# Q turned on VectorE in 32x32 squares instead of on TensorE, for half of the groups, and one piece of a late split moved

## The chip, the cores and the metric

The kernel runs on one core of a Trainium2 chip. The metric is the device time of one execution in microseconds; lower is better. The profile is of one execution, taken by the hardware profiler, with the core's five instruction streams: PE (TensorE; PEld is its weight load), DVE (VectorE), ACT (ScalarE), POOL (GpSimd) and SP (SyncE, which here only issues DMAs).

## The reference

A delta-rule attention, then two feed-forward parts on its output:

```
q, k, v: (4, 8, 768, 48)   beta: (4, 8, 768)
k_n = k / (norm(k) + 1e-6);  state = 0
for t in range(768):
    y[t]  = q[t] @ state
    v_old = k_n[t] @ state
    state = state + beta[t] * outer(k_n[t], v[t] - v_old)
x = y laid out as (3072, 384)
x = (s * relu(x @ w_in)**2 + b) @ w_out            # 384 -> 2048 -> 384
e = argmax of the normalised x against 8 expert embeddings, with a softmax gate
out = gate * (relu(x @ w1[e]) @ w2[e])             # 384 -> 1024 -> 384, by expert
```

## The kernel before

The 768 positions are cut into 24 chunks of 32, and these into six groups (`gi` 0 to 5) of four chunks (`s` 0 to 3). Inside a group each chunk takes three steps on PE, with DVE between them: `ks` (state times k and q, tile `ch`, L307), `tx` (tile `u`, L328), and `ku` with `mu` (tiles `ds`, L344, and `ch`, L363). DVE makes `X`, `bdu` and the state `sst` from them. One step is a "hop"; a group has twelve, and each hop is cut in four. While group `gi` runs, the next one, `g2 = gi + 1`, is prepared: its loads are queued, k and q are turned so that the head dimension lies on the partitions (tile `kqt`, one for each chunk), `gram` multiplies k by k and q (tile `gr`, L220), and DVE inverts a 32x32 triangle (`lanes_1` to `lanes_3`, `solve`).

The first feed-forward part (`moe1`, tiles `h`, `r`, `gh`, `gl`, `acc`) is cut into small pieces that fill PE between the hops; its rows are written in the same program order. `attention` keeps a list of items with the hop at which each is due:

```
                for f in (tr_k, tr_q, gram):
                    for s in range(0, HG, 2 if f is gram else 1):
                        add(h, f, g2, s)
                        h += 0.25
```

with `h` starting at 3.25. So the order on PE, DVE, ACT and POOL is the order of the code; the order on SP's queue is set by a scheduler.

`tr_k` (L152) turns k of one chunk: four PE transposes into a PSUM tile `pp`, one ACT copy into `kqt`. It reads `kpad`, which 32 small DMAs fill (L117), and is due at hops 3.25 to 4. `tr_q` (through `tr_n`, L166 and L171) turns q of one head: four PE transposes of 128x112 into `pp`, four ACT copies. It reads `qpad`, filled by eight DMAs for a group (L125), and is due at 4.25 to 5; `gram` follows at 5.25 and 5.5. `qpad` is one buffer, `kpad` and `v` are two.

The last part (L1003, L917) runs over six blocks of 512 tokens, `s_`, each with four quarters `t`. In a quarter PE runs two pieces of the next block's first product (`ffn1`, tile `h`) and the second product of one quarter (`ffn2`, tile `o`). `x2_split` makes the high and low halves `x2h` (ACT, L992) and `x2l` (POOL, L993) of the block after next, in three pieces `m`, each behind a quarter: piece `t - 1` behind quarter `t`. `ffn1` of a block reads the pieces in the order 0, 1, 2.

Of the kernel before, what the change touches and what calls it, by code (L numbers as in the profile page):

```python
# [6 lines left out]
F32 = mybir.dt.float32  # L7
# [7 lines left out]
C = 32  # L15
HG = 4
# [3 lines left out]
def tile_kernel(ctx, tc, q, k, v, beta, w_in, w_out, s_in, b_in, emb, tau, w1, w2, out):  # L20
    nc = tc.nc
    B, H, S, D = q.shape
# [8 lines left out]
    DP = 2 * 64 - 16  # L31
# [6 lines left out]
    NST = NT // ST  # L38
# [5 lines left out]
    att = tc.alloc_tile_pool(name="att", bufs=1, side="right")  # L44
# [40 lines left out]
    qpad = att.tile([128, B, 4, DP], F32, name="qpad")  # L85
# [21 lines left out]
    v_t, kqt_t, mt_t, beta_t, tt_t, gc_t, x_t = {}, {}, {}, {}, {}, {}, {}  # L107
    KQB, MTB = 6, 6
# [37 lines left out]
                    in_=beta[h, 2 * r:2 * r + 2, gi * HG * C:(gi + 1) * HG * C].rearrange("g (n t) -> g n t", t=C))  # L146

    def tr_k(gi, s, eng=None):
        kqt_t[gi, s] = att.tile([128, B, 256], F32, tag="kqt", name="kqt", bufs=KQB)[0:DP]
        pp = ps_pp.tile([128, B, 128], F32, tag="pp", name="pp")  # L150
        for h in range(B):
            nc.tensor.transpose(out=pp[0:DP, h, :], in_=kpad[gi % 2][:, h, s, 0:DP], identity=ident)  # L152
        o = kqt_t[gi, s].rearrange("p h (a x t) -> p (h a) x t", a=2, x=4)[:, :, 0::3, :]
        i = pp[0:DP].rearrange("p h (a x t) -> p (h a) x t", a=2, x=2)
        if eng is nc.vector:
            nc.vector.tensor_copy(out=o, in_=i)
        else:
            nc.scalar.copy(out=o, in_=i)

    def tr_n(gi, h, t, x, engines):  # L160
        if (gi, 0) not in kqt_t:
            for s in range(HG):
                kqt_t[gi, s] = att.tile([128, B, 256], F32, tag="kqt", name="kqt", bufs=KQB)[0:DP]
        pp = ps_pp.tile([128, 4, HG, C], F32, tag="pp", name="pp")
        for r in range(4):
            nc.tensor.transpose(out=pp[0:DP, r].rearrange("p n t -> p (n t)"), in_=t[:, h, r, 0:DP], identity=ident)  # L166
        for s in range(HG):
            o = kqt_t[gi, s][:, h].rearrange("p (a x t) -> p a x t", a=2, x=4)[:, :, x, :]
            i = pp[0:DP, :, s, :].rearrange("p (a x) t -> p a x t", a=2)
            if engines[s % len(engines)] is nc.scalar:  # L170
                nc.scalar.copy(out=o, in_=i)  # L171
            else:
                nc.vector.tensor_copy(out=o, in_=i)
# [3 lines left out]

    def tr_q(gi, h):
        tr_n(gi, h, qpad, slice(1, 3), (nc.scalar,))

    def k_rows(gi, s):
        pp = ps_pp.tile([128, B, DP], F32, tag="pp", name="kr")
        for h in range(B):
            for r in range(4):
                c = r // 2 * 128 + r % 2 * 96
                nc.tensor.matmul(out=pp[32 * r:32 * r + 32, h, :], lhsT=kqt_t[gi, s][:, h, c:c + 32],
                                 rhs=ident[0:DP, 0:DP], start=True, stop=True)
        nc.scalar.copy(out=kpad[gi][:, :, s, :], in_=pp)
# [225 lines left out]
    def attention(more, first):  # L414
        for gi in range(NG):
            items = []

            def add(h, f, *a):
                items.append((h, len(items), f, a))

            if gi == 0:
                add(0, first)
                for i in range(1, 3 * HG - 1):
                    add(i, x_step)
                add(10, x_step)
            if gi + 1 < NG:
                g2 = gi + 1
                sy = [nc.sync]
                if gi:
                    add(0, load_k, g2, sy)  # L430
                    add(0, load_n, g2, qpad, q, nc.sync)
                    add(0, load_beta, g2)
                    add(0, load_v, g2, nc.sync)
                h = 3.25
                if gi:
                    for f in (tr_k, tr_q, gram):
                        for s in range(0, HG, 2 if f is gram else 1):
                            add(h, f, g2, s)
                            h += 0.25
                else:  # L440
                    add(99, second_places)
                    for f in (tr_k, tr_q, gram):
                        for s in range(0, HG, 2 if f is gram else 1):
                            add(99 if f is tr_k and s < 2 else 100, f, 1, s)
                if gi:
                    for f, a in ((lanes_1, ()), (lanes_2, ()), (lanes_3, ()), (scale_v, (0, nc.vector)),
                                 (scale_v, (1, nc.vector))):
                        add(h, f, g2, *a)
                        h += 0.25
                    he = 11.25  # L450
                    for j in range(C - 1):
                        add(h + (he - h) * j / (C - 1), solve, g2, j)
                    add(he + 0.25, lanes_out, g2)
                else:
                    add(100, router_setup_a2)
                    add(200, lanes_1, 1)
                    add(200, lanes_2, 1)
                    add(200, lanes_3, 1)
                    add(201, scale_v, 1, 0, nc.vector)
                    add(201, scale_v, 1, 1, nc.vector)  # L460
                    add(201, router_setup_b)
                    for j in range(C - 1):
                        add(301 if j % 3 == 2 else 300, solve, 1, j)
                    add(400, lanes_out, 1)
            items.sort(key=lambda x: (min(x[0], 300) if x[0] > 100 else x[0], x[1]))

            def due(t):
                while items and items[0][0] <= t:
                    it = items.pop(0)
                    it[2](*it[3])  # L470

            hops = 0
            for s in range(HG):
                for _ in dstep(gi, s, more):
                    for i in range(4):
                        due(hops + i / 4)
                        st["hop"] += 0.25
                        st["gi"], n = gi, 4 * hops + i
                        w = [(2 if gi == 1 else 1.5) if x >= 23 else 1 for x in range(n, 4 * NS)]
                        st["left"] = sum(w) / w[0]  # L480
                        yield
                    hops += 1
            while items:
                it = items.pop(0)
                it[2](*it[3])
                if it[0] >= 100:
                    yield PREP[it[0]]
        st["hop"] += 100
# [311 lines left out]
    with tc.manual_schedule(engines={ET.PE, ET.DVE, ET.Activation, ET.Pool}):  # L800
# [28 lines left out]
        for s in range(HG):  # L829
            gram_first(0, s, ga)  # L830
            if s % 2:
                for g in range(2):
                    o = gc_t[0][:, :, g, s - 1:s + 1, :]
# [11 lines left out]
        for h in range(B):  # L845
            tr_q(0, h)
# [137 lines left out]
        def x2_split(s_, m):  # L984
            if m == 0:
                xr_t[s_] = xs_t[s_]
                xs_t[s_] = (p2.tile([128, KD, ST], F32R, tag="x2h", name="x2h", bufs=2),
                            p2.tile([128, KD, ST], F32R, tag="x2l", name="x2l", bufs=2))
            xr = xr_t[s_]
            xh, xl = xs_t[s_]  # L990
            o = xh[:, m].rearrange("p (u t) -> p u t", u=NTS)
            nc.scalar.copy(out=o, in_=xr[:, :, m, :])  # L992
            nc.gpsimd.tensor_tensor(  # L993
                out=xl[:, m].rearrange("p (u t) -> p u t", u=NTS), in0=xr[:, :, m, :],
                in1=o.bitcast(F32), op=ALU.subtract)
# [159 lines left out]
        for s_ in range(NST):  # L1155
            if s_ + 2 < NST:
                x2_load(s_ + 2)
            for t in range(NTS):
                if s_ + 1 < NST:
                    ffn1(s_ + 1, 2 * t)  # L1160
                    ffn1(s_ + 1, 2 * t + 1)
                ffn2(s_, t)
                if s_ + 2 < NST and t:
                    x2_split(s_ + 2, t - 1)
                if (s_, t) == (0, 0):
                    router2b()
                for _ in range(2):
                    if nr < NTILE:
                        router3(nr)
                        nr += 1  # L1170
                if nr == NTILE:
                    router4()
                    nr += 1
                    pair_load(0)
                if s_ == NST - 1 and t < NTS - 1:
                    for f in range(KF2 // 2):
                        if t < 2:
                            pair_1(t * KF2 // 2 + f)
                    if t == 2:
                        pair_2()  # L1180
                        pair_out()
                        pair_last()
# [39 lines left out]
```

## Time and profile before

| | us |
|---|---|
| median of 3 runs (lowest, highest) | 921.82 (917.24, 922.56) |
| the profiled execution | 918.63 |
| its span, first to last instruction | 916.8 |
| PE busy in the span | 839.4 (92%) |
| DVE busy | 465.3 (51%) |
| ACT busy | 458.4 (50%) |
| POOL busy | 61.9 (7%) |

The busy times say which engine is full on the whole. The sums behind them are made against the profiled execution: 918.63 us, of which 1.83 us lie outside the span.

### The profile page before, as it was taken

The page shows a single profiled execution, that of the slowest core. Times are in us where ns is not written, and L with a number is a line of the kernel's source. Part 1 is how long each engine was busy: PE and PEld are TensorE (multiplying, and loading weights), DVE is VectorE, ACT ScalarE, POOL GpSimd, SP SyncE. Part 2 cuts the span into 40 slices and gives each one's busy share as a digit, 9 for nine tenths or more (in the row PEclk, how much of TensorE's full clock was granted, in tenths as well). Part 3 has the DMA queues.
Part 4 walks back from the last instruction along what each step waited for, and adds up shares of the span by engine and source line. Part 5 has one row for each costly group of instructions (what it writes and reads, how often), then busy time and mean ns, then how long its engine had stood idle before and what let it go on. Part 6 is the DMA issues. An engine that isn't in the chain of part 4 may idle for free. (4 is left out here: it accounts for less than half of the span.)

```text
span 916.8 us, 27694 instructions
## 1 busy us (share of the span) xinstructions
PE 839.4 (92%) x12090; PEld 770.5 (84%) x12090; DVE 465.3 (51%) x1051; ACT 458.4 (50%) x861; POOL 61.9 (7%) x71
## 2 busy tenths in 40 slices
PE   6467797876999999999999999999999999999996
PEld 4345686775989999999999999999997889889895
DVE  2979588669537942795368632225215423321101
ACT  1544646733575567565756566678653222222211
POOL 5115400000000000000000000000001011011000
PEclk7557899877999999999999999999999999999999
DMA  8683114211220222022000000015002910132000
GB/s 162 195 310 65 28 26 75 48 23 25 47 57 4 47 44 54 3 41 49 20 4 20 3 19 2 19 34 157 19 1 53 56 61 18 60 122 102 26 26 27
DMA packets 115593, 49.42 MB, mean 54 GB/s; under 512 B 89943, under 2 KB 112144, under 8 KB 115472
## 3 DMA queue, kind: packets, MB, share of 16 engines
q1 hardware_dynamic: 108560, 46.44, 22.4%
q10 hardware_dynamic: 6336, 1.18, 0.9%
q8 instruction: 95, 1.56, 0.7%
q14 instruction: 26, 0.21, 0.1%
q0 software_dynamic: 576, 0.02, 0.1%
HBM read 38.06 MB, written 9.74 MB: 52 GB/s over the span
## 5 line engine op out<-in xcount | busy, mean ns | idle before, releaser
L672 PE MATMUL acc<-gh,wp 128*128 128x256 f32 x1056 | 145.4, 284 | 0.0
L672 PEld LDWEIGHTS acc<-gh,wp 128*128 128x128 f32 x1056 | 132.6, 192 | 1.4
L635 ACT ACTIVATE r<-h 128x512 f32<-128x512 f32 x96 | 57.7, 601 | 130.5 <-PE h L627 103.4
L627 PE MATMUL h<-xh,wp 128*128 128x256 f32 x576 | 118.7, 289 | 2.4 <-ACT r L635 1.2
L627 PE MATMUL h<-xhl,wp 128*128 128x256 f32 x720 | 102.2, 287 | 0.0
L627 PEld LDWEIGHTS h<-xh,wp 128*128 128x128 f32 x576 | 94.5, 191 | 3.7 <-ACT r L635 1.6
L920 DVE SCALAR_TENSOR_TENSOR hl<-h,hh 128x512 fp32r<-128x512 f32 x46 | 31.8, 690 | 121.0 <-ACT hh L919 121.0
L649 DVE TENSOR_TENSOR gl<-r,gh 128x512 fp32r<-128x512 f32 x88 | 60.3, 685 | 62.4 <-ACT gh L647 62.4
L627 PEld LDWEIGHTS h<-xhl,wp 128*128 128x128 f32 x720 | 90.4, 189 | 1.1
L627 PE MATMUL h<-xl,wp 128*128 128x256 f32 x288 | 81.0, 281 | 0.0
L672 PE MATMUL acc<-gl,wp 128*128 128x256 f32 x528 | 76.3, 280 | 1.1 <-issue 1.1
L646 ACT ACTIVATE r<-r,b_sb,s_sb 128x512 f32<-128x512 f32 x88 | 72.0, 818 | 2.2
L377 ACT COPY x<-ch 32x384 f32<-32x384 f32 x96 | 45.2, 471 | 48.6 <-PE ch L363 47.5
L672 PEld LDWEIGHTS acc<-gl,wp 128*128 128x128 f32 x528 | 67.8, 190 | 1.3 <-issue 1.2
L289 DVE TENSOR_TENSOR T<-T,tmp 128x31 f32<-128x31 f32 (+15 forms) x186 | 65.1, 350 | 6.4
L993 POOL TENSOR_TENSOR x2l<-xr,x2h 128x512 fp32r<-128x512 f32 x15 | 19.4, 1291 | 719.4 <-DVE L L1090 592.7
L286 DVE TENSOR_TENSOR tmp<-A,T 128x31 f32<-128x31 f32 (+15 forms) x186 | 64.6, 348 | 5.0
L1003 PE MATMUL o<-w2h,hh 128*128 128x384 f32 x184 | 62.6, 340 | 0.0
L636 ACT ACTIVATE r<-r 128x512 f32<-128x512 f32 x96 | 60.7, 632 | 3.1
L1003 PE MATMUL o<-w2h,hl 128*128 128x384 f32 x184 | 62.2, 338 | 0.0
L1003 PE MATMUL o<-w2l,hh 128*128 128x384 f32 x184 | 62.1, 337 | 0.0
L1007 ACT ACTIVATE o<-o,gate 128x384 f32<-128x384 f32 x24 | 14.0, 582 | 94.1 <-PE o L1003 85.3
(215 smaller groups left out, 1437.9 us busy)
## 6 DMA issues: line engine op xcount, KB each, us to landing
wr<-in_moe_w_in SPq DMA_DIRECT2D x16, 384.0 KB
wr<-in_moe_w_out SPq DMA_DIRECT2D x8, 768.0 KB
v<-in_v SPq DMA_DIRECT2D x192, 24.0 KB
x2d<-x2s SPq DMA_DIRECT2D x24, 192.0 KB
out<-o SPq DMA_DIRECT2D x24, 192.0 KB
kpad<-in_k SPq DMA_DIRECT2D x160, 24.0 KB
qpad<-in_q SPq DMA_DIRECT2D x40, 96.0 KB
xr<-x2d SPq DMA_DIRECT2D x5, 768.0 KB
```

The source lines that it names most:

```text
L286: nc.vector.tensor_tensor(out=tmp, in0=A[:, j + 1:, j:j + 1].to_broadcast([128, m, j + 1]), in1=T[:, j:j + 1, 0:j + 1].to_broadcast([128, ...
L289: nc.vector.tensor_tensor(out=T[:, j + 1:, 0:j + 1], in0=T[:, j + 1:, 0:j + 1], in1=tmp, op=ALU.subtract)
L377: nc.scalar.copy(out=x_t[gi][pb:pb + C, :, r * 96:(r + 1) * 96].rearrange("p h (g e) -> p h g e", g=2), in_=y[32 * rr:32 * rr + 32, :, :, ...
L627: nc.tensor.matmul(out=h[:, f, :], lhsT=wi_(w, 2 * j + f, m), rhs=x[:, m, :], start=(m == 0 and i == 0), stop=(m == KD - 1 and i == 2))
L635: nc.scalar.activation(out=r, in_=h, func=AF.Relu)
L636: nc.scalar.activation(out=r, in_=r, func=AF.Square)
L646: nc.scalar.activation(out=r, in_=r, func=AF.Identity, scale=s_sb, bias=b_sb)
L649: later.append((step[0] + 11, lambda: nc.vector.tensor_tensor(out=gl, in0=r, in1=gh.bitcast(F32), op=ALU.subtract)))
L672: nc.tensor.matmul(out=acc[:, m * TT:(m + 1) * TT], lhsT=wo_(w, 2 * j + f, m * 128, 128) if kk else wx_(2 * j + 1, 2 * j + f, m * 128), rh ...
L920: nc.vector.scalar_tensor_tensor(out=hl, in0=ps, scalar=0.0, in1=hh.bitcast(F32), op0=ALU.max, op1=ALU.subtract)
L993: nc.gpsimd.tensor_tensor(out=xl[:, m].rearrange("p (u t) -> p u t", u=NTS), in0=xr[:, :, m, :], in1=o.bitcast(F32), op=ALU.subtract)
L1003: nc.tensor.matmul(out=ps, lhsT=h[:, sl], rhs=w[:, f, :], start=(f == 0 and i == 0), stop=(f == KF2 - 1 and i == 2))
```

## The change

For groups of index 3, 4 and 5 the q of a group is no longer loaded as eight DMAs of all 128 positions. `load_qb` loads each head in four bands: a band is 32 partitions of `qpad` (one half of the head pair `g`, one half `b` of the 48 dimensions), with the 32 positions of a chunk on the partitions and 32 or 16 of the dimensions as columns. That is 16 DMAs a head, 64 a group. `qpad` is seen as three slots, so head 3 shares a slot with head 0. `tr_qb` turns a head with four DVE transposes, one for each chunk, straight into `kqt`: no `pp` tile, no PE transpose and no ACT copy. Heads 0 to 2 are due at hops 3.75, 4 and 4.25, head 3 at hop 5; its load is put in at hop 4.25. `tr_k` starts at hop 2.75 in these groups instead of 3.25; `gram` stays at 5.25. In the last part the third piece of `x2_split` follows quarter 2, together with the second piece, and no longer quarter 3.

```
+    qn = qpad.rearrange("p h r d -> p (h r d)")[:, 0:3 * HG * 128].rearrange(
+        "p (h s r d) -> p h s r d", h=3, s=HG, r=4)
+    kqf_t = {}
+
+    def load_qb(gi, h):
+        for g in range(2):
+            for b in range(2):
+                w = min(32, D - 32 * b)
+                for s in range(HG):
+                    t = (gi * HG + s) * C
+                    nc.sync.dma_start(
+                        out=qn[32 * (2 * g + b):32 * (2 * g + b) + 32, h % 3, s, :, 0:w],
+                        in_=q[h, g::2, t:t + C, 32 * b:32 * b + w].rearrange("r t d -> t r d"))
+
+    def tr_qb(gi, h):
+        for s in range(HG):
+            o = kqf_t[s][:, h].rearrange("p (a x t) -> p a x t", a=2, x=4)[:, :, 1:3, :]
+            nc.vector.transpose(out=o, in_=qn[:, h % 3, s].rearrange("p (a x) d -> p a x d", a=2))
...
-                    add(0, load_n, g2, qpad, q, nc.sync)
+                    if g2 < 3:
+                        add(0, load_n, g2, qpad, q, nc.sync)
+                    else:
+                        for x in range(3):
+                            add(0, load_qb, g2, x)
+                        add(4.25, load_qb, g2, 3)
...
                 if gi:
-                    for f in (tr_k, tr_q, gram):
+                    if g2 > 2:
+                        h = 2.75
+                    for f in (tr_k, tr_qb if g2 > 2 else tr_q, gram):
                         for s in range(0, HG, 2 if f is gram else 1):
+                            if f is tr_qb and s == 3:
+                                h = 5
                             add(h, f, g2, s)
                             h += 0.25
...
                 ffn2(s_, t)
-                if s_ + 2 < NST and t:
-                    x2_split(s_ + 2, t - 1)
+                if s_ + 2 < NST:
+                    for m in ((), (0,), (1, 2), ())[t]:
+                        x2_split(s_ + 2, m)
```

On PE, while group 4 is prepared (`gi` 3), this stood around `tx` and the q turns before; `kpad` rows are `tr_k`, `qpad` rows `tr_q`:

```order
L672 MATMUL acc<-gl,wp_2569 128x256 x6
L152 MATMUL pp<-ident,kpad_103 112x128 x4
L627 MATMUL h<-xhl,wp_1957 128x256 x9
L328 MATMUL u<-X,tt 32x48 x32
L152 MATMUL pp<-ident,kpad_103 112x128 x4
L627 MATMUL h<-xhl,wp_1957 128x256 x3
L696 MATMUL lg<-x2s 128x136 x6
L627 MATMUL h<-xhl,wp_1957 128x256 x6
L166 MATMUL pp<-ident,qpad 112x128 x4
L672 MATMUL acc<-gh,wp_1976 128x256 x9
L166 MATMUL pp<-ident,qpad 112x128 x4
L672 MATMUL acc<-gh,wp_1976 128x256 x3
```

The same place on PE now:

```order
L701 MATMUL acc<-gl,wp_2569 128x256 x6
L656 MATMUL h<-xhl,wp_1957 128x256 x9
L348 MATMUL u<-X,tt 32x48 x32
L656 MATMUL h<-xhl,wp_1957 128x256 x3
L725 MATMUL lg<-x2s 128x136 x6
L656 MATMUL h<-xhl,wp_1957 128x256 x6
L701 MATMUL acc<-gh,wp_1976 128x256 x12
```

And the stretch on PE that begins two pieces earlier, where the k turns stand now:

```order
L701 MATMUL acc<-gl,wp_2471 128x256 x6
L153 MATMUL pp<-ident,kpad_103 112x128 x4
L656 MATMUL h<-xhl,wp_1947 128x256 x9
L327 MATMUL ch<-sst,kqt 64x48 x32
L153 MATMUL pp<-ident,kpad_103 112x128 x4
L656 MATMUL h<-xhl,wp_1947 128x256 x9
L153 MATMUL pp<-ident,kpad_103 112x128 x4
```

The q turns are gone and the twelve `acc` rows stand together; the first k turn stands in front of the `h` piece ahead of `ch`, where it stood behind the `h` piece after `ch`.

On DVE, the same preparation, from `X` to the mask of `gram`, before:

```order
L313 TENSOR_TENSOR X<-v,ch 128x384 x2
L649 TENSOR_TENSOR gl<-r,gh 128x512
L333 TENSOR_TENSOR bdu<-u,par 128x384 x2
L649 TENSOR_TENSOR gl<-r,gh 128x512
L699 TENSOR_TENSOR sq_5493<-lg,ident 128x256
L702 COPY LG<-lg 128x16
L703 TENSOR_REDUCE SS<-sq_5493 128x2
L352 TENSOR_TENSOR sst<-ds,sst 112x4x96 x2
L649 TENSOR_TENSOR gl<-r,gh 128x512
L204 TENSOR_TENSOR mt<-gr,mask_su 128x8x32 x4
```

And now, from the `gl` behind `X`:

```order
L678 TENSOR_TENSOR gl<-r,gh 128x512
L199 STREAM_TRANSPOSE kqt<-qpad 128x2x64 x4
L353 TENSOR_TENSOR bdu<-u,par 128x384 x2
L199 STREAM_TRANSPOSE kqt<-qpad 128x2x64 x4
L678 TENSOR_TENSOR gl<-r,gh 128x512
L728 TENSOR_TENSOR sq_5577<-lg,ident 128x256
L731 COPY LG<-lg 128x16
L732 TENSOR_REDUCE SS<-sq_5577 128x2
L199 STREAM_TRANSPOSE kqt<-qpad 128x2x64 x4
L372 TENSOR_TENSOR sst<-ds,sst 112x4x96 x2
L199 STREAM_TRANSPOSE kqt<-qpad 128x2x64 x4
L678 TENSOR_TENSOR gl<-r,gh 128x512
```

Each head is a block of four transposes: one ahead of `bdu`, one behind it, one ahead of `sst` and, for head 3, one behind `sst`.

On SP, from the loads of group 3 (`v`, `kpad`) to those of group 4, before:

```order
L135 DMA v<-in_v 32x4x48 x19
L117 DMA kpad_104<-in_k 32x4x48 x32
L135 DMA v<-in_v 32x4x48 x13
L688 DMA x2d<-x2s 128x3x128 x2
L125 DMA qpad<-in_q 128x4x48 x8
L924 TENSOR_LOAD esel
L924 ISA x2
L144 DMA beta<-in_beta 8x1x32 x16
L135 DMA v<-in_v 32x4x48 x7
```

And now, up to the second band of group 4's q:

```order
L135 DMA v<-in_v 32x4x48 x19
L117 DMA kpad_104<-in_k 32x4x48 x32
L135 DMA v<-in_v 32x4x48 x13
L192 DMA qpad<-in_q 32x4x32 x4
L192 DMA qpad<-in_q 32x4x16 x4
L192 DMA qpad<-in_q 32x4x32
L717 DMA x2d<-x2s 128x3x128 x2
L192 DMA qpad<-in_q 32x4x32 x3
L192 DMA qpad<-in_q 32x4x16 x4
L192 DMA qpad<-in_q 32x4x32 x4
L192 DMA qpad<-in_q 32x4x16 x4
```

Behind `v` stand first the sixteen loads of group 3's head 3, nine ahead of the `x2d` stores and seven behind them, and then the 48 loads of group 4's heads 0 to 2, still ahead of the next `beta` and `v`.

## Rows read from the trace of the kernel before

**Rows 1.** Busy time by engine in one preparation; last columns: PEclk, DMA share, GB/s.

```profile
260.00:356.00 96.00, 94.29 (x1799) 90.55 (x1798) 58.92 (x142) 59.69 (x115) 0.00 (x0) 1.00 0.19 36
```

**Rows 2.** Timeline of PE, group 4: start, length, what, count.

```profile
342.34 1.54 PE L672 MATMUL acc<-gh,wp 128*128 128x256 f32 x12
343.72 0.84 PE L672 MATMUL acc<-gl,wp 128*128 128x256 f32 x6
344.40 1.22 PE L627 MATMUL h<-xhl,wp 128*128 128x256 f32 x9
...
356.21 0.60 PE L166 MATMUL pp<-ident,qpad 128*112 128x128 f32 x4
356.57 1.30 PE L672 MATMUL acc<-gh,wp 128*128 128x256 f32 x9
...
358.06 0.60 PE L672 MATMUL acc<-gh,wp 128*128 128x256 f32 x3
358.49 0.85 PE L672 MATMUL acc<-gl,wp 128*128 128x256 f32 x6
```

**Rows 3.** Timeline of PE in the four stalls of the last part, the first of them.

```profile
744.03 0.49 PE L917 MATMUL h<-x2h,w1h 128*128 128x512 f32 x1
745.38 0.50 PE L917 MATMUL h<-x2l,w1h 128*128 128x512 f32 x1 [0.84 <-POOL x2l L993]
745.71 0.40 PE L917 MATMUL h<-x2h,w1l 128*128 128x512 f32 x1
745.95 0.39 PE L917 MATMUL h<-x2h,w1h 128*128 128x512 f32 x1
```

**Rows 4.** Timeline of POOL and of ACT at the splits.

```profile
744.06 1.26 POOL L993 TENSOR_TENSOR x2l<-xr,x2h 128x512 fp32r<-128x512 f32 x1 [7.15 <-ACT x2h L992]
```

```profile
769.86 0.61 ACT L992 CAST x2h<-xr 128x512 fp32r<-128x512 f32 x1
771.43 0.60 ACT L919 ACTIVATE hh<-h 128x512 fp32r<-128x512 f32 x1 [0.95 <-PE h L917]
```

**Rows 5.** DVE's transposes by line: count, ns min/median/max, first and last start.

```profile
L241 DVE STREAM_TRANSPOSE A<-gc x6: 1936/1992/2078, 20.7 to 466.4; 128x1024 f32<-128x1024 f32 x6
```

```profile
L276 DVE STREAM_TRANSPOSE nmc<-nm x6: 204/205/205, 26.7 to 474.5; 128x32 f32<-128x32 f32 x6
```

**Rows 6.** Timeline of DVE, groups 3 and 4; in brackets the idle time before.

```profile
251.47 0.68 DVE L649 TENSOR_TENSOR gl<-r,gh 128x512 fp32r<-128x512 f32 x1
```

```profile
353.40 1.02 DVE L333 TENSOR_TENSOR bdu<-u,par 128x384 f32<-128x384 f32 x2 [5.01 <-PE u L328]
...
361.70 1.02 DVE L352 TENSOR_TENSOR sst<-ds,sst 112x384 f32<-112x384 f32 x2 [5.13 <-PE ds L344]
```

**Rows 7.** Timeline of SP's queue from group 3's q to group 4's k.

```profile
179.37 5.93 SPq L125 DMA_DIRECT2D qpad<-in_q  x8
200.08 10.38 SPq L144 DMA_DIRECT2D beta<-in_beta  x16
215.99 10.32 SPq L135 DMA_DIRECT2D v<-in_v  x19
226.41 18.45 SPq L117 DMA_DIRECT2D kpad<-in_k  x32
...
258.05 1.24 SPq L688 DMA_DIRECT2D x2d<-x2s  x2
...
304.54 3.74 SPq L135 DMA_DIRECT2D v<-in_v  x7
...
322.95 17.05 SPq L117 DMA_DIRECT2D kpad<-in_k  x32
```

**Rows 8.** DMA issues with a time to landing: KB each, median us.

```profile
beta<-in_beta POOLq DMA_DIRECT2D x16, 1.0 KB, 3.7
```

**Rows 9.** Timeline of PE, group 3: the unit ahead of the k turns, and gram.

```profile
248.17 1.22 PE L627 MATMUL h<-xhl,wp 128*128 128x256 f32 x9
```

```profile
268.15 1.48 PE L220 MATMUL gr<-kqt 48*32 48x64 f32 x128
```

More of the change, by code (lines that the diff above doesn't have):

```diff
@@ L148, in tr_k @@
     def tr_k(gi, s, eng=None):
-        kqt_t[gi, s] = att.tile([128, B, 256], F32, tag="kqt", name="kqt", bufs=KQB)[0:DP]
+        kqf_t[s] = att.tile([128, B, 256], F32, tag="kqt", name="kqt", bufs=KQB)
+        kqt_t[gi, s] = kqf_t[s][0:DP]
         pp = ps_pp.tile([128, B, 128], F32, tag="pp", name="pp")
```

## The prediction

> **What bounds the kernel now.** I read the busy times by engine first, then PE's timeline, then the queues that feed it. In a whole preparation (260 to 356 us) PE is busy 94.3 of 96 us at a granted clock of 1.00, full speed (2.4 GHz); DVE is busy 58.9, ACT 59.7 [rows 1]. So in the groups that the change touches, PE's own instructions set the time, and what is taken from PE there shortens the kernel unless a new wait takes its place. In the last part PE stands still at four places for one reason: the second matmul of the third piece of a block waits for POOL's `x2l` [rows 3]. These two, PE time and that wait, are what the change can win. What can take it back is SP, which issues its DMAs one behind the other [rows 7].
>
> **Part 1, the q turns leave PE.** A turn is four transposes. Twelve `acc` matmuls without turns take from 342.34 to 343.72, 1.38 us. The same twelve, cut by two turns, take from 356.21 to 358.49, 2.28 us [rows 2]. So a turn costs PE 0.45 us, of which 0.36 is its own slot (356.21 to 356.57) and the rest the matmul behind it. Four turns a group, three groups: 12 x 0.45 = **5.4 us**, all of it in a stretch where PE is full. The lower bound is the slots alone, 12 x 0.36 = 4.3. The ACT copies behind the turns also go; ACT is not the bound and I count nothing for them.
>
> **What DVE gets.** 16 transposes a group of 128 columns on 128 partitions. No row has this size, but two lie around it: 32 columns take 205 ns, 1024 take 1992 [rows 5]. A line through them gives 1.80 ns a column and 0.38 us for one, 1.5 us for a head's block of four, 6.0 us a group. The bounds are 0.2 and 2.0 us; I take the line, since both rows are the same operation on the same type. Block by block: head 0's stands ahead of `bdu`, before which DVE is idle 5.01 us; head 2's ahead of `sst`, idle 5.13 [rows 6]. Head 1's delays `gl`, which PE reads two units later, and the small sums of the router, by 1.5 us. The cover is that idle time on DVE; it is three times the block, so the cost is nothing. Without it each block would delay `ds` or the next `ch` by up to 1.5 us.
>
> A rule of the Trainium skill speaks against this part: "VectorE: DVE Perf Modes", in its rules for kernel authors, sends a 128x128 transpose to TensorE and only a 32x32 one to DVE, and its section on the three transpose paths puts DVE at 311 ns and TensorE at 390 for 128x128 in bf16. Taken with its figures the DVE blocks would cost 4 x 0.31 us, an estimate from that page, and the sum stays as it is. By the rows above a turn on PE is in fact the cheaper one (0.45 us against 1.5), so the trace agrees with the rule; what decides here is which engine is full. Where the rule would win is rival C.
>
> **What SP gets.** 64 DMAs a group instead of 8. Each has 32 partitions by 4 runs, the form of the k loads, which go out at 17.05 / 32 = 0.53 us apiece; the eight old q loads took 5.93 / 8 = 0.74 each, a part of it waiting [rows 7]. I take 0.53 and keep 0.74 as the upper bound; the lower is 0.5, since nothing here goes out faster. Two chains hang on this.
>
> First, group 3's q stands ahead of `beta`, `v` and k. 48 loads from 179.37 end at 204.9; sixteen `beta` (10.4) at 215.3; `v` starts at 215.99 in any case, held by DVE's last use of the buffer [rows 7]. So the k loads start where they did, at 226.41, and are out at 244.86. No row times an SP load to landing; the nearest is 3.7 us on POOL's queue [rows 8], and it gives 248.6. The first k turn now stands where 248.17 is, ahead of the matmuls that begin there [rows 9]. That is a wait of 0.4 us; bounds 0 and, at 0.74 a load, about 10. I take **0.4**. In group 4 the same chain starts when head 3's squares free their slot, near 266.5, and ends at 266.5 + 25.4 + 10.4 = 302.3, against `v` held until 304.54, less the 1.8 us that PE is earlier by then: level. Its k, 32 loads from 322.95, is out at 340.0, and the first turn stands at 344.40 [rows 2, 7], both earlier by the same amount: no wait.
>
> By the Trainium skill, "DMA: Bandwidth & Descriptors", on the anatomy of a DMA, the fixed cost of one is some 2.0 us, measured there on the other path, POOL's. With it k lands at 246.9, and the 0.4 falls away; the sum would be 0.4 us less. This case's 3.7 is longer; no run so far shows SP's.
>
> Second, head 3. Its slot is free when head 0 is turned: `gl` ends at 252.15 [rows 6], the first square 0.38 later, 252.5. Nine loads, 4.8 us, to 257.3; then the `x2d` stores, which wait for ACT and go out at 258.05 [rows 7], to 259.0; then seven, to 262.7; landed by 266.4. `gram` stood at 268.15 [rows 9] and is 1.8 earlier, 266.3, but takes head 3 last of its first chunk, half a us in, and the load for that chunk is the fourth of the seven, landed by 264.8. No wait; at 0.74 a load it would be some 3 us a group.
>
> **Part 2, k turned half a hop earlier.** The same sixteen transposes and four copies, ahead of `ks` in place of behind it; no DMA of its own. On ACT they pass one `r` and `gh`. It costs only what the k loads above cost.
>
> **Part 3, the third piece of the split.** Between 744.03 and 745.71 PE makes two steps that take 0.24 each elsewhere (745.71 to 745.95): 1.68 - 0.48 = 1.2 us lost [rows 3]. POOL starts the piece at 744.06 [rows 4], too late by its whole 1.26 us. There are four such stalls of the same length, one for each of blocks 2 to 5: **4.8 us**. One quarter earlier is some 8 us earlier, so nothing of the wait is left; what is late next is the matmul pipe itself. The extra ACT cast, 0.61 us, stands ahead of `hh`, before which ACT is idle 0.95 [rows 4]; were that cover gone, it would cost 0.6 in each of four blocks. The next load of `xr` then moves ahead of one store of `out` on SP, and that store waits for POOL's two pieces, some 3 us; its buffer is needed again two quarters later.
>
> **Sum.** 5.4 + 4.8 - 0.4 = 9.8 us; 918.63 - 9.8 = **908.8** for the profiled execution. That execution lies 3.2 us under the median of the runs shown and 1.4 over the lowest. I give 909, nearer to the sum than to the median. The bounds of the terms: 4.3 and 5.4 for the turns, 4.8, and 0 to 3 for small waits, so 906 to 913, 1 to 3 us more if the runs lie where the median does.
>
> **Rivals.**
>
> A. *SP runs late by a little.* The loads of head 3 or of k land 1 to 2 us behind their reader in each of the three groups, and the q half nets out: 3 x 1.8 = 5.4 back. For it: the two chains above are level with their limits within 1 us. Against: the packets are of the same kind as k's. Only the last part's gain is left: 918.6 - 4.8 = 914.
>
> B. *SP's queue becomes the bound; slower than before.* Everything on it is in order, so a late q pushes `v` and k, and PE stops at the first k turn, with every hop behind it. It decides at (215.99 - 10.4 - 179.4) / 48 = 0.55 us a load; each 0.1 us above adds 4.8 us in group 3, and nearly that in group 4. If the loads waited as the first old ones did (0.74), that is 9 us in group 3, 8 in group 4 and 3 x 3 for head 3: 26, so 908.8 + 26 = 935. For it: 64 issues take 34 us of a preparation in which SP already issues some 45. Against: k's row, and that group 5 has no successor.
>
> C. *DVE's blocks are not covered* (the rule above). If the squares ran behind their time, the two blocks ahead of `bdu` and `sst` would stand in the way of PE's `ds` and `ch`: 3 x 2 x 1.5 = 9 us, 908.8 + 9 = 918. Idle times of 5 us before both [rows 6] speak against it.
>
> D. *The stall in the last part doesn't go*, because `x2h` or `xr` ends later instead: 908.8 + 4.8 = 913.6. Against: nothing else was late there.
>
> **How the numbers follow.** Forecast 0.60, A 0.20, B 0.08, C 0.04, D 0.08. About 1% is what a measurement of this kernel can tell from no change: 912.6 and 931.0 around the median. The forecast lies under 912.6 with most of its mass (0.55), A, C and D are within, B is above. So faster 0.56, same 0.36, slower 0.08. The range takes the forecast with its small waits and A, C and D's nearer part: 904 to 917; 904 is the sum without waits, with the lowest run as its base, and some 2 us for effects of the ACT copies that are not counted.
>
> **What would show it.** 48 fewer q transposes on PE and 48 DVE transposes near 0.38 us; q loads on SP near 0.53 us apiece; no PE wait on DMA ahead of the first k turn of groups 3 to 5 beyond 0.4 us, and none of `gram` on DVE's `kqt`; one stall on `x2l` left where there were five with that of the first block. The prediction is wrong if the q loads go out slower than 0.55 us, if landing takes over 4 us, or if `bdu` or `sst` start late.

## The result, and the profile after

The changed kernel takes 904.6 us (median of 4 runs, 903.24 to 907.8) against 920.18 for the kernel before: ratio 0.9831, 95% interval 0.9805 to 0.9857. Timed once more it takes 907.34 (6 runs, 905.71 to 910.16) against 919.27: 0.9871, 0.9849 to 0.9894. The profiled execution takes 903.99 us, with a span of 902.3; before it was 918.63 with 916.8. Forecast: 909, a gain of 9.8 us on the profiled execution; measured: 14.6 on the profiled execution, 15.6 and 11.9 by the two pairs of medians. The mean granted clock of TensorE is 0.947 against 0.948 before, so the clock has no part in it.

The page of the changed kernel, busy time by engine, and one preparation of 96 us, to be read against [rows 1]:

```profile
PE 831.4 (92%) x12042; PEld 765.2 (85%) x12042; DVE 475.1 (53%) x1099; ACT 449.8 (50%) x813; POOL 61.8 (7%) x71
...
257.00:353.00 96.00, 95.23 (x1812) 91.67 (x1805) 64.70 (x167) 56.99 (x99) 0.00 (x0) 1.00 0.23 39
```

PE has 48 matmuls and 8.0 us less than before, ACT 48 copies less, DVE 48 transposes more. In the preparation PE is fuller than before and still at full clock: nothing of the removed work came back in this stretch as a wait.

PE's timeline in group 4, where the cut chain of [rows 2] stood, and gram behind it:

```profile
352.89 1.54 PE L701 MATMUL acc<-gh,wp 128*128 128x256 f32 x12
354.27 0.84 PE L701 MATMUL acc<-gl,wp 128*128 128x256 f32 x6
...
358.99 1.48 PE L240 MATMUL gr<-kqt 48*32 48x64 f32 x128
360.40 1.30 PE L701 MATMUL acc<-gh,wp 128*128 128x256 f32 x9
361.64 0.63 PE L240 MATMUL gr<-kqt 48*32 48x64 f32 x30
362.87 1.18 PE L240 MATMUL gr<-kqt 48*32 48x64 f32 x98 [0.60 <-issue]
```

The twelve `acc` matmuls take 1.38 us (352.89 to 354.27) where they took 2.28.

DVE: the squares' line (ns min/median/max), then its timeline in group 4, against [rows 5, 6]:

```profile
L199 DVE STREAM_TRANSPOSE kqt<-qpad x48: 266/270/306, 252.2 to 451.6; 128x128 f32<-128x128 f32 x48
```

```profile
345.50 0.89 DVE L199 STREAM_TRANSPOSE kqt<-qpad 128x128 f32<-128x128 f32 x4
350.47 1.02 DVE L353 TENSOR_TENSOR bdu<-u,par 128x384 f32<-128x384 f32 x2 [4.08 <-PE u L348]
...
357.03 1.02 DVE L372 TENSOR_TENSOR sst<-ds,sst 112x384 f32<-112x384 f32 x2 [2.59 <-PE ds L364]
357.97 0.88 DVE L199 STREAM_TRANSPOSE kqt<-qpad 128x128 f32<-128x128 f32 x4
```

A head's block is 0.9 us, not 1.5. `bdu` and `sst` still wait for PE, with 4.08 and 2.59 us of idle time left of 5.01 and 5.13. Head 3's block stands right behind `sst` without a wait for its loads.

SP's queue, from group 3's q to group 4's k, against [rows 7]:

```profile
179.46 28.55 SPq L192 DMA_DIRECT2D qpad<-in_q  x48
208.11 10.39 SPq L144 DMA_DIRECT2D beta<-in_beta  x16
218.59 9.71 SPq L135 DMA_DIRECT2D v<-in_v  x19
228.40 16.76 SPq L117 DMA_DIRECT2D kpad<-in_k  x32
...
321.01 17.57 SPq L117 DMA_DIRECT2D kpad<-in_k  x32
```

A load costs 28.55 / 48 = 0.595 us of the queue, more than the 0.53 taken and more than the 0.55 at which rival B was to decide. `v` starts 2.6 us later than before, k 2.0 later; but k is out at 245.16 against 244.86, since its 32 loads now follow at 0.52 apiece (0.58 before). PE there, against [rows 9]:

```profile
247.13 0.85 PE L701 MATMUL acc<-gl,wp 128*128 128x256 f32 x6
247.81 0.60 PE L153 MATMUL pp<-ident,kpad 128*112 128x128 f32 x4
```

The first k turn starts when `gl` is through, without a wait: k had landed 2.7 us behind its issue at the latest.

In the last part the third piece of a block is read without a stop, where [rows 3] had 1.35 us between two starts:

```profile
734.35 0.39 PE L946 MATMUL h<-x2h,w1h 128*128 128x512 f32 x1
734.58 0.40 PE L946 MATMUL h<-x2l,w1h 128*128 128x512 f32 x1
734.82 0.39 PE L946 MATMUL h<-x2h,w1l 128*128 128x512 f32 x1
```

The table gives the length of each stretch of PE's timeline against the same stretch of the kernel before (minus: shorter); the bounds are steps of PE, in us on the clock of the kernel before. 230.9 is the first `ks` of group 2, during which group 3 is prepared; 277.3, 372.5 and 468.2 are the first `ks` behind the `gram` of groups 3, 4 and 5; 692.9 is a step early in the last part. So the row of a group is the stretch that ends with its preparation.

| stretch | forecast | after | repeat |
|---|---|---|---|
| start to 230.9 | 0 | -0.4 | +0.8 |
| group 3, 230.9 to 277.3 | -1.4 | -2.97 | -2.95 |
| group 4, to 372.5 | -1.8 | -2.18 | -1.81 |
| group 5, to 468.2 | -1.8 | -2.70 | -2.93 |
| 468.2 to the last part, 692.9 | 0 | -1.5 | -0.2 |
| last part | -4.8 | -4.78 | -4.80 |
| sum | -9.8 | -14.5 | -11.9 |

So the last part came out as forecast; the groups won 7.7 to 7.9 where 5.0 were forecast; and the two profiles differ by 2.5 us at the beginning and between 468 and 693, where the change does nothing. The surplus in the groups is what needs a cause.

### The profile page after: what moved, and what is told of

Read it like the earlier page. It is cut to its first block, busy times and chain, and to the rows that moved or that the text cites. A ratio compares the mean times of both kernels' runs of the same rounds, so it can differ in the third digit from the quotient of the medians.

```text
span 902.3 us, 27807 instructions
## 1 busy us (share of the span) xinstructions
PE 831.4 (92%) x12042; PEld 765.2 (85%) x12042; DVE 475.1 (53%) x1099; ACT 449.8 (50%) x813; POOL 61.8 (7%) x71
```

## The experiments

### Each half alone

The changed kernel without part 3:

```
-                if s_ + 2 < NST:
-                    for m in ((), (0,), (1, 2), ())[t]:
-                        x2_split(s_ + 2, m)
+                if s_ + 2 < NST and t:
+                    x2_split(s_ + 2, t - 1)
```

> The q half of the change alone: bands, squares and the earlier k turn as changed, the third piece of the split where it was. Theory T (turns leave a full PE, and the four stalls are an independent 4.8 us): the four stalls on x2l are back and the time lies 4.8 us above the changed kernel, near 909.5, that is some 10 us under the kernel before. Rival (the two halves share a gain, or the split is worth more than its stalls show): 912 or more, or under 907.

The kernel before with part 3 alone (the same lines the other way round):

> The kernel before with the third piece of the split moved and nothing else. Theory T: the four stalls of 1.2 us go, 4.8 us under the kernel before, near 915.4. Rival (the piece moves the wait to another place, a cast ahead of hh or a store behind xr): less than 2.5 us.

Measured: q alone 910.07 us, ratio 0.9909 (0.9888 to 0.993), 8.2 us less than before; the split alone 914.02, ratio 0.9959 (0.9942 to 0.9976), 4.2 less. Both are near what theory T expected, 909.5 and 4.8 less. The halves add up to 12.4; the changed kernel won 15.6 at first and 11.9 when it was timed again. PE's waits on `x2l` (us in total, times, longest) with q alone, which are those of the kernel before:

```profile
PE h L946 <- POOL x2l L1022: 4.2, 5, 0.8
```

and in the changed kernel:

```profile
PE h L946 <- POOL x2l L1022: 0.8, 1, 0.8
```

Four stalls of five are gone and nothing else is late in their place: rival D is out. With q alone one more line stands among the waits, and in PE's timeline it is this one:

```profile
PE pp L153 <- DMA kpad<-in_k: 1.5, 1, 1.5
```

```profile
342.27 0.29 PE L153 MATMUL pp<-ident,kpad 128*112 128x128 f32 x1 [1.51 <-DMA kpad<-in_k]
```

The k loads of group 4 were out at 340.82 in that run (323.13 + 17.69): SP is at its edge, and runs differ by what happens there. The granted clock stayed at 1.00 through this wait.

### Where the surplus in the groups is from

Three kernels leave the q turns on PE and change one thing around them. First, the half hop alone (part 2):

```
                     for f in (tr_k, tr_q, gram):
+                        if g2 > 2:
+                            h = {tr_k: 2.75, tr_q: 4.25, gram: 5.25}[f]
```

> The kernel before with part 2 alone: the k turns of groups 3 to 5 start at hop 2.75, the q turns stay on PE at 4.25, one buffer and eight loads, the split stays as it is. Theory T (the half hop wins nothing by itself, it only makes room for head 3's chain; what the changed kernel wins beyond the two terms, the 1.1 us gap ahead of acc in group 3 and some 1 us in gram, comes with the q turns and their ACT copies leaving): within 1 us of the kernel before, from 230.9 to 580.4 us between 0 and -1, and the 1.1 us gap still there in group 3. Rival (the room between the k turns and gram is what gram won by, since its wait was on ACT's k copies or on the order of the code): 1.5 to 2.5 us less than before, the gap gone and gram's pieces at 1.41 us.

Second, the turns stay on PE and their copies go to DVE:

```
-        tr_n(gi, h, qpad, slice(1, 3), (nc.scalar,))
+        tr_n(gi, h, qpad, slice(1, 3), (nc.vector,) if gi > 2 else (nc.scalar,))
```

> The kernel before, but the 16 copies behind the q turns of groups 3 to 5 run on DVE and not on ACT; all turns stay on PE. It asks where the gain beyond 12 x 0.45 us comes from. Theory T: gram of groups 4 and 5 no longer waits for ACT's copy of head 3, some 0.3 us each, in all 0.5 to 1 us under the kernel before; the turns stay. Rival R (it is the relief of ACT that shortens the groups, the turns cost less than a slot each): 3 us or more under the kernel before.

Third, every q transpose of these groups is issued twice:

```
-        for r in range(4):
+        for r in [x for x in range(4) for _ in range(2 if gi > 2 else 1)]:
```

> The kernel before with each PE transpose of q in groups 3 to 5 issued twice, so 24 turns instead of 12; copies as they were. It measures the price of a turn's PE slots by itself. Theory T: 12 x 0.36 to 0.45 us more, 4.3 to 5.4 us over the kernel before, with PE moved by 1.4 to 1.8 us in each of the three groups. Rival R (PE has room around the turns): under 2 us more.

Measured: half hop alone 919.62, ratio 1.0008 (0.9991 to 1.0025); copies on DVE 919.36, 1.0009 (0.9992 to 1.0027); turns twice 922.34, 1.0044 (1.002 to 1.0068). So neither part 2 nor the copies' engine wins anything by itself. For the copies on DVE 0.5 to 1 us was expected, which the time doesn't show; why is said below. The doubled turns cost only 3.3 us in the three groups where 4.3 to 5.4 were expected, which looked like a miss of the price. It isn't. PE's timeline of group 4 with doubled turns shows the eight transposes in a slot of 0.79 us (356.62 to 357.41), 0.43 more than a turn of four takes:

```profile
356.62 1.03 PE L166 MATMUL pp<-ident,qpad 128*112 128x128 f32 x8
357.41 1.29 PE L672 MATMUL acc<-gh,wp 128*128 128x256 f32 x9
```

Twelve times 0.43 is 5.2. The 1.9 that are missing lie where no turn is, in gram and behind it: 1.0 of them in pauses that the trace puts down to "issue", that is to nothing it shows (2.43 us in the three groups where the kernel before has 3.45), and 0.5 in gram's first piece of groups 4 and 5. Of the pauses there are two in the kernel before, in group 3, one inside gram and one inside the `acc` chain behind it:

```profile
270.80 0.31 PE L220 MATMUL gr<-kqt 48*32 48x64 f32 x6
271.68 1.43 PE L220 MATMUL gr<-kqt 48*32 48x64 f32 x122 [0.57 <-issue]
273.03 0.62 PE L672 MATMUL acc<-gh,wp 128*128 128x256 f32 x3
273.49 0.50 PE L672 MATMUL acc<-gl,wp 128*128 128x256 f32 x3
275.13 0.50 PE L672 MATMUL acc<-gl,wp 128*128 128x256 f32 x3 [1.14 <-issue]
```

With doubled turns there is one, at another place:

```profile
272.15 1.40 PE L220 MATMUL gr<-kqt 48*32 48x64 f32 x118
274.47 0.32 PE L220 MATMUL gr<-kqt 48*32 48x64 f32 x10 [0.91 <-issue]
```

Count the matmuls of this stretch from gram's second piece on. Before, the pauses stand behind matmul 6 and behind 6 + 122 + 3 + 3 = 134: 128 apart. Sixteen more transposes ahead of them put the second one behind matmul 118 = 134 - 16, where it is. In groups 4 and 5 the pause stood behind 118 and 102; with 32 and 48 transposes more, behind 86 and 54: both to the matmul. In the changed kernel, with 16 transposes less in each group, it stands behind 26, 30 and 34, which is 20, 40 and 60 later, counted round by 128. (Why 20 and not 16 isn't in the trace; waits that went with the turns may count.) So the places lie 128 matmuls apart, 256 instructions with their weight loads, fixed in PE's stream, and an edit ahead of them moves them. Not every place costs something: 128 ahead of the first pause of group 3 lies in gram's first piece, which runs its 128 matmuls in 1.41 us without a stop. In the half-hop and the split kernels, where the number ahead is nearly the same, both pauses of group 3 are still there (0.61 and 1.03; 0.49 and 1.14); in the changed kernel and its repeat the one behind gram is gone: 20 later, by the count, its place is where the fifteen `h` matmuls behind gram end and `ch` begins, and no stop is seen there.

This accounts for most of the surplus. Pauses in the three groups: 3.45 us before (0.57, 1.14, 0.70, 1.04), 2.02 after (0.77, 0.60, 0.65), 1.67 in the repeat. The size at one place changes from run to run, but the two sets stay apart: with the turns as they were 3.5 to 4.5 us (kernel before, split alone, half hop alone, copies on DVE), with the turns gone 1.5 to 2.0 (changed kernel, repeat, and those with `beta` on POOL and with the squares twice). What is gone in every one of the second set is the 1.03 to 1.14 us behind gram in group 3. With copies on DVE the pauses come to 4.5, 1.1 more than before, which is why that kernel shows no gain.

And gram's first piece waited for the copies of head 3's turn in groups 4 and 5: it is 1.70 and 1.76 us long where it takes 1.41 without. In group 4 the copies run on ACT while gram has begun:

```profile
364.07 1.78 PE L220 MATMUL gr<-kqt 48*32 48x64 f32 x128
364.49 0.77 ACT L171 COPY kqt<-pp 112x128 f32<-112x128 f32 x4
```

The trace puts 0.2 us of PE's idle time inside gram down to this copy in each of the two groups, and none in group 4 with the copies on DVE, where the piece takes 1.52.

Turns 5.4, pauses 1.4, copies 0.6: 7.4 of the 7.85 us that the groups won. The other 0.4 stay open, and the split between pauses and copies is a sum over single traces, not a measurement of its own.

### The half hop

The changed kernel with the k turns back at hop 3.25. Three heads' squares follow at 4, 4.25 and 4.5, since they need k's tiles:

```
-                    if g2 > 2:
-                        h = 2.75
...
-                            if f is tr_qb and s == 3:
-                                h = 5
+                            if f is tr_qb:
+                                h = (4, 4.25, 4.5, 5)[s]
```

> The changed kernel with the k turns back at hops 3.25 to 4 and the squares of heads 0 to 2 at 4, 4.25 and 4.5 (a quarter hop later, since they need the k turn's tile); head 3 stays at hop 5 and gram at 5.25. It asks what the half hop is worth. Theory T: the turns cost PE the same wherever they stand, so the changed kernel's time within 2 us; head 3's load starts about 2 us later and is still landed. Rival (the earlier k turn is what keeps head 3's chain off gram): PE waits for DVE's squares ahead of gram, 1 to 3 us a group, 3 to 9 us over the changed kernel.

Measured: 915.83 us, ratio 0.9974 (0.995 to 0.9998), 8 to 11 over the changed kernel: the rival's side, and more. PE, DVE and SP in group 3:

```profile
266.29 0.72 PE L240 MATMUL gr<-kqt 48*32 48x64 f32 x48
269.82 1.28 PE L240 MATMUL gr<-kqt 48*32 48x64 f32 x80 [2.81 <-DVE kqt L199]
```

```profile
258.00 0.88 DVE L199 STREAM_TRANSPOSE kqt<-qpad 128x128 f32<-128x128 f32 x4
...
269.45 1.39 DVE L199 STREAM_TRANSPOSE kqt<-qpad 128x128 f32<-128x128 f32 x4 [4.42 <-DMA qpad<-in_q]
```

```profile
257.94 1.20 SPq L715 DMA_DIRECT2D x2d<-x2s  x2
259.27 38.37 SPq L192 DMA_DIRECT2D qpad<-in_q  x64
```

Head 0's squares stand behind `bdu` at 258.00 and not ahead of it at 252.2. Its slot comes free that much later, head 3's sixteen loads go out behind the `x2d` stores and not around them, and gram stands still until they have landed. Gram's first piece takes 4.2 to 4.7 us in place of 1.41. Behind the wait of group 3 the granted clock is 0.50 (1.2 GHz) from 271.0 to 273.2, and nine `acc` matmuls take 2.2 us in place of 1.2, so that wait cost more than its length. Without the half hop the q half of the change would win nothing: 3.2 us under the kernel before is less than the split alone wins.

### DVE's cover

Every square issued twice:

```
-            nc.vector.transpose(out=o, in_=...)
+            for _ in range(2):
+                nc.vector.transpose(out=o, in_=...)
```

> The changed kernel with every square transpose issued twice: 96 in place of 48, so a block takes 1.75 us and not 0.88. Theory T (DVE has idle time of 1.6 to 4 us ahead of bdu and sst in the changed kernel): the changed kernel's time within 1.5 us. Rival C (DVE's blocks are on the path): 3 groups x 2 blocks x 0.9 = 5 us over the changed kernel.

Measured: 907.9 us, ratio 0.9862 (0.9819 to 0.9906). From 230.9 to 580.4 us it wins 7.0 where the changed kernel wins 8.1 and its repeat 7.7. The blocks take 2.27 us and not the 1.75 expected, more than twice the real ones, and cost about 1 us in three groups where rival C has 5. `bdu` still has 2.71 us of idle time ahead of it in group 3; `sst` has none left, but what PE waits for is another thing, ACT's `r` in group 3:

```profile
264.80 0.60 ACT L665 ACTIVATE r<-h 128x512 f32<-128x512 f32 x1 [4.87 <-DVE SS L733]
265.45 1.33 PE L657 MATMUL h<-xhl,wp 128*128 128x256 f32 x9 [0.66 <-ACT r L665]
```

ACT waited for `SS`, the router's small sum, which head 1's block delays. In the changed kernel ACT waits 3.48 us for it there and PE does not wait. So at 0.9 us the blocks are covered and rival C is out; the cover that ends first is the one behind head 1, not those ahead of `bdu` and `sst`.

### SP's room

Three kernels put more on the queue. Head 2's loads issued twice, sixteen more ahead of `beta`, `v` and k:

```
-                        for x in range(3):
+                        for x in (0, 1, 2, 2):
                             add(0, load_qb, g2, x)
```

> The changed kernel, in which the sixteen loads of head 2 are issued twice, so that 64 and not 48 small loads stand ahead of beta, v and k in each of groups 3 to 5. Head 3's loads and its chain stay as they are. Theory T (SP's queue has room for the 48 loads and hardly for more, since one load takes 0.6 us of it): beta, v and k go out 16 x 0.6 = 9.5 us later in group 3. The first k turn of group 3 stood right behind its k (issue out at 245.16, turn at 247.81), so PE waits 6 to 10 us ahead of it on kpad; in group 4 v was held by DVE to 303.16 and beta ended at 301.89, so some 8 us there, of which k's own turn (344) gives back what lies between 338.6 and it, so 3 to 6 us; in group 5 v is held longer and nothing is seen. Together 10 to 16 us over the changed kernel, 914 to 921. Rival (the queue has room, landing and not issue sets the time of k): within 3 us of the changed kernel.

Every band in two loads of half the runs (128 a group):

```
-                    nc.sync.dma_start(out=qn[..., h % 3, s, :, 0:w], in_=q[h, g::2, ...])
+                    for y in range(2):
+                        nc.sync.dma_start(out=qn[..., h % 3, s, 2 * y:2 * y + 2, 0:w],
+                                          in_=q[h, g + 4 * y:g + 4 * y + 3:2, ...])
```

> The changed kernel with every band load cut in two by runs: 128 DMAs a group of half the size, the same bytes. The band loads go out 0.59 us apart; if that is a price of the issue, 96 of them take 57 us ahead of group 3's beta, v and k. Rival B's mechanism, forced: k is out some 28 us later than now in group 3, about as late in group 4, and PE stops ahead of the k turns; the whole 40 to 70 us over the changed kernel. If the pace follows bytes or packets instead: no change.

Group 2 prepared in the same way too:

```
-                    if g2 < 3:
+                    if g2 < 2:
...
-                    if g2 > 2:
+                    if g2 > 1:
```

> The changed kernel with the bands and squares for group 2 as well. By the mechanism of rival B: in that group the hops go by faster, k's loads are out at 145 us, 48 band loads take until 176 and nineteen loads of v and the beta of the next group stand between them and head 3's loads, so head 3 is out near 205 us while gram stands at 185: PE waits 15 us or more, 10 to 20 us over the changed kernel. Rival (SP has room there too): 2 us under the changed kernel for four more turns gone.

One run each: 920.18, 968.93 and 932.07 us, 13 to 64 over the changed kernel. The first lies among the runs of the kernel before (917.5 to 922.9), so all of the gain is gone; the other two are 50 and 13 us slower than that kernel. The first two lie in what was expected; the third is 25 to 28 over the changed kernel and not 10 to 20. With sixteen more loads, SP and PE in group 3, and PE in group 4:

```profile
235.62 16.26 SPq L117 DMA_DIRECT2D kpad<-in_k  x32
```

```profile
246.77 0.38 PE L153 MATMUL pp<-ident,kpad 128*112 128x128 f32 x2
249.49 0.32 PE L153 MATMUL pp<-ident,kpad 128*112 128x128 f32 x1 [2.33 <-DMA kpad<-in_k]
253.39 0.46 PE L153 MATMUL pp<-ident,kpad 128*112 128x128 f32 x1 [3.58 <-DMA kpad<-in_k]
...
353.68 0.43 PE L153 MATMUL pp<-ident,kpad 128*112 128x128 f32 x1 [3.61 <-DMA v<-in_v]
```

A turn takes the four heads in the order in which their k is loaded, so PE's steps show the loads landing one by one: heads 0 and 1 are there, head 2 comes at 249.49, head 3 at 253.39. Its last load was out at 251.88: 1.5 us to the first use. With q alone the wait in group 4, shown above, gives the same (340.82 to 342.27). Groups 3 and 4 are 8.3 and 7.4 us longer than in the changed kernel; group 5 is as long as there. Not all of that is the wait. Behind it PE runs at a granted clock of 0.50 (1.2 GHz), after 6.8 us in which it was busy for 0.9. First the stretch (its length, PE's busy time, granted clock, DMA share, GB/s), then the steps in it:

```profile
253.50:257.50 4.00, 4.00 (x74) 0.50 0.24 39
```

```profile
253.51 2.27 PE L656 MATMUL h<-xhl,wp 128*128 128x256 f32 x9
255.71 1.96 PE L327 MATMUL ch<-sst,kqt 48*64 48x48 f32 x64
```

These two steps take 1.26 and 1.08 us in the changed kernel and 2.20 and 1.89 here: 1.8 of the 8.3 us are the clock. Group 4 shows the same behind its wait. With halves, 96 loads take 52.06 us:

```profile
178.17 52.06 SPq L193 DMA_DIRECT2D qpad<-in_q  x96
```

That is 0.54 each at half the bytes: the price is by the issue. With group 2 added, one wait of gram for the squares takes 22.7 us (15 or more was expected), since head 3's loads go out behind everything else (among those that begin at 198.01):

```profile
PE gr L240 <- DVE kqt L199: 22.7, 1, 22.7
```

### Beta off the queue, and the fifth stall

The changed kernel with `beta` of groups 3 to 5 on POOL's queue, and block 1's split in two steps:

```
-                    add(0, load_beta, g2)
+                    add(0, load_beta, g2, nc.gpsimd if g2 > 2 else None)
...
-            if f >= KF2 - KD:
-                x2_split(1, f - KF2 + KD)
+            for m in {KF2 - 3: (0,), KF2 - 2: (1, 2)}.get(f, ()):
+                x2_split(1, m)
```

> The changed kernel with two edits: the sixteen beta loads of groups 3 to 5 go out on POOL's queue, so that SP has 10.4 us more room in each group; and block 1's split of the last part, which the change left as it was, gets its second and third piece together, one place earlier. Theory T: the changed kernel no longer waits on k, so the room on SP wins nothing by itself; the fifth stall on x2l (1.2 us) goes, as the four others went: 0.8 to 1.2 us under the changed kernel, 903 to 904 against 904.6. Rival: POOL's issues stand in the way of its part of the preparation or of x2l, or beta lands later than v and the solve waits for it: 1 to 4 us slower than the changed kernel, with a DVE or PE wait on beta in groups 3 to 5.

and the changed kernel beside it:

> The changed kernel itself once more, beside the run with beta on POOL and on the same chip, so that the two can be compared. All theories: 903 to 907; its trace tells whether the 1.1 us gap ahead of acc in group 3 and the 1.3 us between 590 and 693, which no part of the change accounts for, come back (then they are the run's and not the change's) or stay away.

Measured: 906.57 us (906.24 to 907.36), ratio 0.9858 (0.9835 to 0.9882), beside 907.34 for the changed kernel: 0.8 less, with intervals that overlap, so not told apart by the times. In the trace the fifth stall is gone, but PE gains only 0.1 us by it up to its last step: the next thing behind it is late too, DVE's `hl`:

```profile
703.36 0.50 PE L946 MATMUL h<-x2h,w1h 128*128 128x512 f32 x1 [0.38 <-DVE hl L949]
```

To the end of the span the last part wins 5.43 where the repeat wins 4.80, but 0.5 of these 0.6 us lie behind PE's last step, which the edit doesn't touch. So the expected 0.8 to 1.2 us for the fifth stall are not there. The repeat has a wait on k in group 4:

```profile
343.21 0.30 PE L153 MATMUL pp<-ident,kpad 128*112 128x128 f32 x1 [0.48 <-DMA kpad<-in_k]
```

With `beta` off SP there is none. In the repeat the pause behind gram stays away, and the 1.3 us that the first profile won between 468 and 693 don't come back: those were that run's own.

## Why the prediction was right

The likeliest case is the one that happened: the turns and the stalls win what was said, and nothing new is late that costs much. The time lies 0.6 us inside the lower end of the range on the first timing and 3.3 on the second. The profiled execution is 4.8 us under the sum; 1.9 of these are that run's own, at the beginning and between 468 and 693, and 2.9 lie in the groups. Half of the 2.9 come from pauses that no step of the prediction has; that they went down and not up when the turns left is luck. Step by step:

- **The turns, 5.4 us: right.** The chain went from 2.28 to 1.38 us, 0.45 a turn; from 230.9 to group 3's gram, and from the `ks` behind each gram to the next, PE gains 1.8, 1.7 and 2.0 us. The doubled turns give 0.43 for the slot alone.
- **The third piece, 4.8 us: right**, 4.78 and 4.80. "What is late next is the matmul pipe itself" holds too for these four; at the fifth stall it would have been DVE's `hl`.
- **DVE costs nothing: right.** The squares took 0.27 us, not the 0.38 of the line between the two sizes. The Trainium skill's rule ("VectorE: DVE Perf Modes", rules for kernel authors) agrees with the cost of a block, 0.9 us on DVE against 0.45 on PE, and did not decide.
- **SP: two sizes wrong, in opposite directions.** A load took 0.60 and not 0.53; the landing took 1.5 us from the end of the issue, not 3.7, the row of another queue. The figure of "DMA: Bandwidth & Descriptors" in the Trainium skill (anatomy of a DMA), some 2.0 us, is said there for POOL's path and was nearer all the same: from the start of the last issue, half a us earlier, it is 2.0 here. By that k came about 1 us ahead of its reader in group 3; in group 4 it came up to 1.5 us late in some runs. The wait of 0.4 us that the sum has in group 3 is not there.
- **Rival B's point of 0.55 us was wrong**, and with it a sign that the prediction named: it was to be wrong if the loads went out slower than that. They did, and it was not. The point was worked out from the start of `v`; the loads passed it and cost nothing, because between `v` and k's reader there was room (k's own loads that follow faster, and the shorter landing). B's mechanism is true: sixteen loads more, and PE stops at the first k turn.
- **Part 2 "costs only what the k loads cost": right, and not enough.** It was priced as a cost and not as what carries head 3's chain; taken away, it costs 8 to 11 us. "Land without a wait" for head 3 rested on head 0's squares standing ahead of `bdu`, which only the earlier k turns allow.
- **What the sum left out** is the 2.4 us in the groups beyond the turns. 0.6 is gram's wait for ACT's copies, of which the range had "some 2 us ... not counted". 1.4 is the pauses of PE's stream, which no step had. 0.4 stays open.

## What to carry to other kernels

Moving work from a full engine to an idle one won its slot on the full one here, though it took twice as long on the other, because everything behind each block had room; look for that room behind every block, down to the next reader on the full engine, in the timeline and not in totals. The first room to go, when the blocks were doubled, was one off the main chain. When a change trades few DMAs for many, price the queue by the issue, and follow the lateness to the instruction that reads the data, not to the next DMA: the room between is part of the sum. When a wait is several us long, look at the granted clock behind it before dividing the loss by the cause. When a kernel gains a us that no step explains, count the instructions to the pauses that the trace calls "issue" before looking for a cause in the work.

## What was not expected of the hardware

PE's stream pauses at places 128 matmuls apart, and what a pause costs depends on what stands there and ahead of it: 0.2 to 1.4 us inside gram's second piece, whose matmuls follow at 11 ns (128 in 1.41 us), nothing or up to 0.6 in its first piece, and mostly nothing among 128x256 matmuls of 115 ns, unless gram has just run. The instruction queue on the profile's page of the changed kernel fits that (packets, MB, share of 16 engines):

```profile
q8 instruction: 95, 1.56, 0.7%
```

95 packets of 16 KB for 24,084 PE instructions (matmuls and weight loads), 253 for each. The Trainium skill says in "Runtime: NRT & Kernel Launch", instruction fetch mechanics, that instructions come in blocks of 16 KiB, 256 of them, and that a crossing is mostly hidden. The period agrees; inside gram it is not hidden. The traces bear out more than the period: in the kernel before, the changed kernel, its repeat and the one with doubled turns all fourteen pauses of groups 3 to 5 end 2.2 to 2.8 us behind a packet of this queue, whatever their length (0.2 to 1.1 us). So the pause is the wait for such a block, as far as traces can tell; the page of the profile doesn't say that this queue is PE's, and no run here took the pause away.
